# Expert slots for token blocks in groups of 8, 6, 2, 2, 2 and 1, with fewer counting products, later writes of the norms and an earlier read of the diagonal blocks

## The chip, the core and the metric

The kernel runs on one core of a Trainium2 chip. The metric is the time of one execution in device microseconds (us); lower is better. The engines are TensorE (PE; its weight loads are listed as PEld), VectorE (DVE), ScalarE (ACT), GpSimd (POOL) and SyncE (SP), which here only issues DMAs. Each engine runs its instructions in program order.

## The reference, cut to what matters

A delta-rule linear attention runs over 4 batches of 8 heads with 768 steps of width 48. Its output is 3072 tokens of 384 features, and a mixture of 8 experts is applied to them, each token going to the one expert with the largest gate logit.

```python
for t in range(S):
    y[:, :, t] = einsum('bhd,bhde->bhe', q[:, :, t], state)
    v_old = einsum('bhde,bhd->bhe', state, k_n[:, :, t])
    state = state + beta_t * einsum('bhd,bhe->bhde', k_n[:, :, t], v[:, :, t] - v_old)
x = y.transpose(0, 2, 1, 3).reshape(3072, 384)
logits = x @ w_gate
expert_idx = argmax(logits, axis=1)
gate_w = softmax(logits)[arange(3072), expert_idx]
for e in range(8):
    xe = x[expert_idx == e]
    out[expert_idx == e] = gate_w * (relu(xe @ w1[e]) @ w2[e])
```

## The kernel before, in words

**Blocks and ticks.** Time is cut into chunks of 128 steps, so there are NT = 6 chunks of B = 4 batches: NN = 24 blocks of 128 tokens. Block n is batch n % 4 of chunk n // 4. The main loop has 27 ticks. In tick t four lanes of 32 rows work on the blocks t, t-1, t-2 and t-3 (LAG is 3), each on another quarter of its block. `residual(t)` forms key times state on PE and DVE subtracts it from v (L468). `apply(t)` multiplies by the inverse of a triangular 32x32 matrix (L476), and ACT copies the result (L481). `qpart`, `kpart` and `finish` form the other products (L282, L496, L506, L516). PE, ACT and DVE all take part in each tick, and the next tick's residual needs the state that this tick's copies write.

**The inverses.** `prepare(tb)` and `lanes(tb)` compute on DVE the inverses for all blocks of a chunk, some 27 us of DVE work per chunk. Their steps are handed out by `beside(t, i)`, which is called at seven places (i = 0 to 6) in each tick, so their instructions stand in DVE's queue between those that PE waits for. They read the diagonal 32x32 blocks of a Gram matrix: `diagonal` (L251) writes them to DRAM in two parts of four DMAs, and `gather` (L257) reads them back into the tile `lg`. The list `off` says at which tick and place each is issued. The norms that `prepare` gives are turned by DVE and written by four small DMAs (L352) into `nt_t`, which `scale_v` (L426) reads at the end of the chunk before its use, two or more ticks later.

**Slots.** When block n is finished, `emit_x` (tick n + 4, L546) forms its 128 output rows and gate logits in one PSUM bank, and ACT copies the rows to a tile `row` (L547). Blocks are gathered into groups of w: 4 for the blocks 0 to 11, 2 for 12 to 19, and 1 for the last four. `emit_slots` is a generator that takes one step per call. It finds each token's expert on DVE (L565 to L583), counts on PE with a triangular product (L588) and one small product for every pair of blocks in a group (L591), adds the running base on DVE (L597, L598), forms the slot numbers (L610 to L626), writes the rows with one DMA per two blocks to `xn` in token order (L630), and lets POOL scatter each block's rows to its experts' slots in `xg` by an indirect DMA (L640). The list `fine` holds the generators; `beside` steps only the first of them, 17 times per tick. For groups of 4 the scatters go two per tick, at place 3 or later of the two ticks that follow.

**The rest.** From tick 20 on expert weights are loaded and split into two parts of lower precision (L677, L678). After the ticks, from about 310 us on, the experts' products run on PE alone (L789, L799, L1101). Rows of an expert beyond 448 would be done in a loop that these inputs do not enter.

Of the kernel before, what the change touches and what calls it, by code (L numbers as in the profile page):

```python
# [8 lines left out]
F32 = mybir.dt.float32  # L9
F32R = mybir.dt.float32r  # L10
BF16 = mybir.dt.bfloat16
I32 = mybir.dt.int32
# [6 lines left out]
B, H, S, D = 4, 8, 768, 48  # L19
C = 128  # L20
NT = S // C
# [4 lines left out]
E = 8  # L26
# [16 lines left out]
def deltanet_moe(ctx, tc, qT, kT, kr, v, beta, w_gate, w1, w2, out):  # L43
# [30 lines left out]
    def constants():  # L74
        nc.gpsimd.memset(esel, 0.0)
        for p in range(NP):
            for a in range(2):
                r, x = (64 * (a ^ p % 2), a * D)
                nc.gpsimd.tensor_copy(esel[r:r + D, p, x:x + D], ident[r:r + D, r:r + D])
        cmask = lp.tile([128, 128], F32, name="cmask", tag="u", bufs=UB)  # L80
        nc.gpsimd.memset(cmask, 1.0)
        nc.gpsimd.affine_select(out=cmask, in_=cmask, compare_op=ALU.is_gt, fill=0.0, base=0,
                                pattern=[[1, 128]], channel_multiplier=-1)
        nc.gpsimd.tensor_copy(ltri, cmask)
        nc.gpsimd.memset(ones, 1.0)
# [4 lines left out]
        iota(ids, [[-C, B * NT]], int(TOPID), -1)  # L90
# [21 lines left out]
    FINE = (3, 3, 3, 2, 2, 2, 2)  # L112
    W0 = 42
    WD = {1: 12, 2: 15, 3: 14, 4: 3}
    W1 = 4
    W4 = 12
    DM2 = 0
    DEF = 2
    AH = 3
# [139 lines left out]
    def put_off(at, tb, b):  # L259

        if tb == 1:
            diagonal(tb, b)
            if b == B - 1:
                gather(tb)
            return
        off.append((at, lambda: diagonal(tb, b)))
        if b == B - 1:
            off.append(((at[0], 3), lambda: gather(tb)))

    def due(t, i):  # L270

# [44 lines left out]
    def prepare(tb):  # L316
# [168 lines left out]
    def finish(n):  # L485
# [33 lines left out]
        for j in range(2):  # L519
            nc.scalar.copy(out=yt[:, j::2], in_=yp[j])  # L520
        yield
        w = 1 if n >= NN - W1 else 2 if n >= W4 else 4
        j, m = n % w, min(w, 2)
        if j == 0:
            tiles["rows"] = []
            tiles["rl"] = lp.tile([128, w, E], F32, name=f"rl{tb}_{b}", tag=f"rl{w}", bufs=2)
        if j % m == 0:
            pool, tag = (fp, "rowb") if j >= 2 else (rp, "row") if n < NN - 2 else (xq_[0], "row")
            t = pool.tile([128, 2 if n < NN - 2 else 1, ROW], F32, name=f"row{tb}_{b}", tag=tag, bufs=2)
            tiles["rows"].append(t[:, 0:m])  # L530
        xp = emit_x(n, yt, tiles["rows"][-1][:, j % m])
        yield
        nc.vector.tensor_reduce(out=tiles["rl"][:, j], in_=xp[:, :, 2 * D:].rearrange("t p e -> t e p"), axis=AX.X, op=ALU.add)
        if j == w - 1:
            fine.append(emit_slots(tb, b - w + 1, w, tiles["rows"], tiles["rl"]))

    def st_view(b, p):
        t = st_t[b][0:RP, p, :]
# [11 lines left out]
    def emit_slots(tb, b, w, parts, rl):  # L550

        V = nc.vector

        def small(nm, shape, dt=F32):
            return lp.tile(shape, dt, name=f"{nm}{tb}_{b}", tag=f"{nm}{w}", bufs=1 if w > 1 else 2)

        def wide(t):
            return t.unsqueeze(2).broadcast_to([128, w, E])
# [8 lines left out]
        m = w // len(parts)  # L567

        def span(i):
            return slice((b + i * m) * NT + tb, (b + i * m + m - 1) * NT + tb + 1, NT)  # L570
# [4 lines left out]
        cols = slice(b * NT + tb, (b + w - 1) * NT + tb + 1, NT)  # L575
        oh = small("oh", [128, w, E])
        V.scalar_tensor_tensor(out=oh, in0=lm, scalar=0.0, in1=both(rev_e), op0=ALU.is_ge, op1=ALU.mult)
        yield
# [14 lines left out]
        dst = xg if tb * B + b < NN - DEF else xt  # L593
# [10 lines left out]
        if tb * B + b + w == NN - DEF:  # L604

            V.scalar_tensor_tensor(out=base, in0=lim, scalar=float(128 * NG - CAP), in1=base, op0=ALU.add, op1=ALU.max)
        if tb * B + b + w == EU:
# [11 lines left out]
        yield  # L619
        if dst is xt:  # L620

            one = rp.tile([128, CAP - 128 * NG], F32, name=f"one{b}")
            V.tensor_scalar(out=one, in0=last_i, scalar1=sl_all[:, cols], scalar2=None, op0=ALU.is_equal)
            last.append((parts[0][:, 0], one))
        sli = rp.tile([128, w], I32, name=f"sli{tb}_{b}", tag=f"sli{w}", bufs=2)
        V.tensor_copy(sli, sl_all[:, cols])  # L626
        yield
        t1 = t0
        def keep(i):
            nc.sync.dma_start(out=xn.rearrange("(b t p) c -> t p b c", b=B, p=C)[tb, :, b + i * m:b + i * m + m], in_=parts[i])  # L630

        keep(0)
        for j in range(w):
            if w > 1 and j % 2 == 0:
                while tiles["t"] == t1 or tiles["at"] < (2 if w == 2 else 3):
                    yield
                t1 = tiles["t"]
                if j > 0:
                    keep(j // m)
            ins = nc.gpsimd.indirect_dma_start(out=dst, out_offset=bass.IndirectOffsetOnAxis(ap=sli[:, j:j + 1], axis=0),  # L640
                                         in_=parts[j // m][:, j % m], in_offset=None, bounds_check=E * CAP - 1, oob_is_err=False)
            for x in put:
                tc.declare_no_dep(ins.ins, x, reason="slots are distinct rows")
            if w > 1 and j % 2 == 0:
                after(ins, "behind the small products", tiles["few"])
            put.append(ins.ins)
        if tb * B + b + w == EU:
            load_main(0, 0, G0)
        if tb * B + b + w == NN - DEF:
            load_main(0, G0, NG)  # L650

    def run(gen, steps=1):
# [305 lines left out]
    def beside(t, i):  # L958

        tiles["t"], tiles["at"] = t, i  # L960
        due(t, i)
        inverses((STEPS0 if t < B else STEPS)[i], t, i)
        if before and (t, i) >= READY.get(before[0][0], (B * before[0][0] - B, 0)):
            if not run(before[0][1], 3):
                before.pop(0)
        for _ in range(FINE[i] if t < NN - B else 4):
            if fine and not run(fine[0]):
                fine.pop(0)
        for _ in range(WSL.count((t, i))):
            run(W)  # L970
        for _ in range(ES.count((t, i))):
            ahead_step()
# [334 lines left out]
```

## Time and profile before

| | us |
|---|---|
| runs | 525.05, 533.33, 526.01 |
| median | 526.01 |
| the profiled execution, its own time | 532.47 |
| its span, first to last instruction | 530.7 |
| mean granted clock of TensorE in it, of full speed | 0.961 |

Times in the rows below count from the span's start. A row of a timeline, of the chain of waits or of the stretches comes from that one execution, which is 6.46 us above the median of the three runs. Line numbers are those of the kernel before.

### The profile page before, as it was taken

How to read it: one execution, taken by the hardware profiler on the slowest of the kernel's cores; microseconds unless marked ns; L12 is line 12 of the kernel's file. 1: busy time of each engine (PE TensorE's matmuls, PEld its weight loads, DVE VectorE, ACT ScalarE, POOL GpSimd, SP SyncE). 2: the span in 40 equal slices, each digit the busy share in tenths (PEclk: the TensorE clock that was granted, in tenths of full speed). 3: DMA queues.
4: the chain of work that ended last, by engine and by line, in shares of the span. 5: the costliest groups of instructions: out<-in, count | busy, mean ns of one | idle time of the engine just before them, and what ended most of it. 6: DMA issues, size and time to landing. Idle time of an engine off the chain costs nothing.

```text
span 530.7 us, 17441 instructions
## 1 busy us (share of the span) xinstructions
PE 487.4 (92%) x7298; PEld 435.4 (82%) x7298; DVE 344.3 (65%) x1013; ACT 253.8 (48%) x536; POOL 113.1 (21%) x146
## 2 busy tenths in 40 slices
PE   7899999998998978888999899999999999999992
PEld 5755678787887867767888799999999999999991
DVE  2999869798899996455432775565665645575310
ACT  3512557574866736564441454444545434454310
POOL 6010111242331524042122010303021130303111
PEclk8699999998999989798999989999999999999997
DMA  6588738756676455465122667483754638481000
GB/s 214 125 219 249 182 119 219 201 159 177 200 189 182 140 173 149 150 198 145 49 88 90 155 198 174 129 203 123 168 159 131 174 109 180 119 202 62 13 18 26
DMA packets 78317, 79.10 MB, mean 149 GB/s; under 512 B 46985, under 2 KB 65978, under 8 KB 78236
## 3 DMA queue, kind: packets, MB, share of 16 engines
q1 hardware_dynamic: 74780, 68.39, 48.1%
q0 software_dynamic: 3456, 9.57, 4.9%
q8 instruction: 58, 0.95, 0.8%
q14 instruction: 23, 0.19, 0.1%
HBM read 54.25 MB, written 24.37 MB: 148 GB/s over the span
## 4 chain that ended last, share of the span: by engine, by line
PE 60%; DVE 26%; issue 3%; ACT 3%; DMA 3%; SPq 2%; POOL 1%; ACTq 0%; DVEq 0%; POOLq 0%
PE h L789 21%; PE y L799 18%; DVE lw L383 7%; PE y L1101 4%; DVE ta L372 4%; DVE tc L393 3%; PE pq L282 2%; PE xp L546 2%; DVE tc L401 2%; PE ks L476 2%; PE ks L449 2%; PE yp L516 2%; DVE tb L372 2%; PE pg L282 2%; SPq L717 1%
## 5 line engine op out<-in xcount | busy, mean ns | idle before, releaser
L799 PE MATMUL y<-w2h,hx 128*128 128x384 f32 x352 | 93.8, 340 | 2.3 <-DVE hx L793 2.1
L802 POOL DMA_INDIRECT out_dram<-yo,idx x32 | 40.3, 1260 | 203.8 <-ACT yo L1096 116.2
L799 PEld LDWEIGHTS y<-w2h,hx 128*128 128x128 f32 x352 | 64.1, 188 | 3.9 <-DVE hx L793 3.0
L678 DVE TENSOR_TENSOR w2l<-w2r,w2h 128x768 fp32r<-128x768 f32 x32 | 31.4, 983 | 48.6 <-ACT w2h L677 48.1
L481 ACT COPY u<-ks 32x384 f32<-32x384 f32 x96 | 45.1, 469 | 35.0 <-PE ks L476 28.6
L789 PE MATMUL h<-xh,w1l 128*128 128x448 f32 x168 | 61.4, 366 | 0.0
L789 PE MATMUL h<-xl,w1h 128*128 128x448 f32 x168 | 61.3, 365 | 0.0
L789 PE MATMUL h<-xh,w1h 128*128 128x448 f32 x168 | 61.2, 364 | 0.0
L799 PE MATMUL y<-w2l,hx 128*128 128x384 f32 x176 | 59.5, 338 | 0.0
L793 DVE SCALAR_TENSOR_TENSOR hx<-h,hx 128x448 fp32r<-128x448 f32 (+1 forms) x64 | 37.5, 587 | 29.2 <-ACT hx L792 28.5
L792 ACT ACTIVATE hx<-h 128x448 fp32r<-128x448 f32 (+1 forms) x64 | 33.2, 518 | 46.8 <-PE h L789 46.8
L301 POOL TENSOR_SCALAR_AFFINE_SELECT pm<-pm 128x1024 f32<-128x1024 f32 x24 | 27.3, 1136 | 115.6 <-DVE tb L372 35.9
L449 PE MATMUL ks<-st,kt 112*32 112x96 f32 x768 | 43.0, 249 | 1.8 <-issue 1.5
L1096 ACT ACTIVATE yo<-y,gt 128x384 f32<-128x384 f32 x22 | 12.8, 581 | 63.3 <-PE y L799 36.2
L678 DVE TENSOR_TENSOR w1l<-w1r,w1h 128x1024 fp32r<-128x1024 f32 x24 | 29.5, 1230 | 13.3 <-ACT w1h L677 12.8
L449 PEld LDWEIGHTS ks<-st,kt 112*32 112x32 f32 x768 | 31.9, 110 | 6.5 <-issue 2.6
L383 DVE TENSOR_TENSOR lw<-lw,ta 128x31 f32<-128x31 f32 (+7 forms) x96 | 36.7, 382 | 0.2
L476 PE MATMUL ks<-v_all,wt 32*32 32x48 f32 x1536 | 25.9, 209 | 11.3 <-DVE v_all L468 8.4
L476 PEld LDWEIGHTS ks<-v_all,wt 32*32 32x32 f32 x1536 | 21.6, 109 | 17.0 <-DVE v_all L468 11.6
L282 PE MATMUL pg<-kt 48*128 48x128 f32 x384 | 32.3, 317 | 3.2 <-DMA kt<-in_kT_dram 2.0
L547 ACT COPY row<-xp 128x384 f32<-128x384 f32 x24 | 11.5, 479 | 48.3 <-PE xp L546 48.3
L282 PEld LDWEIGHTS pg<-kt 48*128 48x128 f32 x384 | 28.5, 221 | 6.6 <-ACT gg L241 2.3
(162 smaller groups left out, 1055.5 us busy)
## 6 DMA issues: line engine op xcount, KB each, us to landing
w1r<-in_w_dram SPq DMA_DIRECT2D x24, 512.0 KB
w2r<-in_w_dram SPq DMA_DIRECT2D x32, 384.0 KB
xg<-zrow SPq DMA_DIRECT2D x14, 394.0 KB
kt<-in_kT_dram SPq DMA_DIRECT2D x24, 224.0 KB
qt<-in_qT_dram SPq DMA_DIRECT2D x24, 224.0 KB
xr<-xg SPq DMA_DIRECT2D x28, 168.0 KB
xn<-row SPq DMA_DIRECT2D x10, 394.0 KB
ku<-in_kr_dram SPq DMA_DIRECT2D x20, 192.0 KB
```

The source lines that it names most:

```text
L282: ins = nc.tensor.matmul(pg[a][:, p], lhsT=kt[r, p], rhs=xt[r, p], start=True, stop=True, tile_position=(64 * a, 0), skip_group_check=True)
L372: noted(nc.vector.tensor_tensor(out=x, in0=lg[:, rows, c:c + 1].broadcast_to([128, m, w]), in1=lw[:, c:c + 1, cols].broadcast_to([128, m, ...
L383: tiles["mark"] = noted(nc.vector.tensor_tensor(out=y, in0=y, in1=x, op=ALU.subtract))
L449: nc.tensor.matmul(ks[32 * q:32 * q + 32, 2 * p:2 * p + 2, :], lhsT=kt_t[n % KTL][0:RP, p, 32 * q:32 * q + 32], rhs=st_view(n % B, p), sta ...
L476: ins = nc.tensor.matmul(ks[r, h, :], lhsT=tiles[n // B]["wt"][r, n % B * H + h, :], rhs=vn[r, h, :], start=True, stop=True, tile_position ...
L481: nc.scalar.copy(out=uview(n)[r], in_=ks[r])
L678: nc.vector.tensor_tensor(out=lo, in0=src, in1=hi.bitcast(F32), op=ALU.subtract)
L789: nc.tensor.matmul(ps, lhsT=w[:, d, fs], rhs=x_[:, d], start=(n == 0), stop=(n == len(terms) - 1))
L792: nc.scalar.activation(out=hh, in_=ps, func=AF.Relu)
L793: nc.vector.scalar_tensor_tensor(out=hl, in0=ps, scalar=0.0, in1=hh.bitcast(F32), op0=ALU.max, op1=ALU.subtract)
L799: nc.tensor.matmul(ps, lhsT=h(f)[h_], rhs=w2[w][:, f, :], start=(n == 0), stop=(n == len(terms) - 1))
L802: nc.gpsimd.indirect_dma_start(out=out, out_offset=bass.IndirectOffsetOnAxis(ap=idx, axis=0), in_=yo, in_offset=None, bounds_check=N - 1, ...
```

## The change

Five things are edited.

- The blocks are grouped as 8, 6, 2, 2, 2, 1, 1, 1, 1. The groups of 4 that ended with the blocks 3 and 11 are gone; the group that ends with block 7 has eight blocks, the one that ends with block 13 has six. A group may now span two or more chunks, so the columns of `ids`, `sl_all` and `m2_all` are ordered by block. The rows of a group's third and later blocks go to tiles `row1`, `row2`, `row3` with one buffer each, in place of one tile with two buffers.
- Counting takes w products behind the triangular one: product i adds the counts of block i to all later columns at once, by a broadcast operand.
- The scatters of the group of 8 go two per tick in four ticks, those of the group of 6 three per tick in two ticks from place 2 on. `beside` steps all generators in `fine`, not only the first.
- For the chunks from 2 on the four writes of the norms go to `off`, for place 2 of tick 4 tb - 3, instead of being issued as soon as `prepare` ends in tick 4 tb - 4.
- `gather` is issued at place 2 of its tick instead of place 3.

```diff
-    W1 = 4
-    W4 = 12
+    GROUPS = (8, 6, 2, 2, 2, 1, 1, 1, 1)
...
-            off.append(((at[0], 3), lambda: gather(tb)))
+            off.append(((at[0], 2), lambda: gather(tb)))
...
-            for q in range(NB):
-                p = slice(32 * q, 32 * q + 32)
-                nc.sync.dma_start(out=nt_t[p, (B * tb + q) * H:(B * tb + q) * H + 32], in_=sn[p])
+            def spread():
+                for q in range(NB):
+                    p = slice(32 * q, 32 * q + 32)
+                    nc.sync.dma_start(out=nt_t[p, (B * tb + q) * H:(B * tb + q) * H + 32], in_=sn[p])
+
+            if tb < 2:
+                spread()
+            else:
+                off.append(((B * (tb - 1) + 1, 2), spread))
+                off.sort(key=lambda x: x[0])
...
-            pool, tag = (fp, "rowb") if j >= 2 else (rp, "row") if n < NN - 2 else (xq_[0], "row")
-            t = pool.tile([128, 2 if n < NN - 2 else 1, ROW], F32, name=f"row{tb}_{b}", tag=tag, bufs=2)
+            pool, tag = (lp, f"row{j // 2}") if j >= 2 else (rp, "row") if n < NN - 2 else (xq_[0], "row")
+            t = pool.tile([128, 2 if n < NN - 2 else 1, ROW], F32, name=f"row{tb}_{b}", tag=tag, bufs=1 if j >= 2 else 2)
...
-        for j in range(1, w + 1):
-            for i in range(j):
-                nc.tensor.matmul(pp[:, j, :], lhsT=ones, rhs=ohb[:, i], start=False, stop=(i == j - 1),
-                                 skip_group_check=True)
+        for i in range(w):
+            nc.tensor.matmul(pp[:, i + 1:w + 1, :], lhsT=ones, rhs=ohb[:, i:i + 1].broadcast_to([128, w - i, E]), start=False,
+                             stop=(i == w - 1), skip_group_check=True)
...
+        few = 3 if w == 6 else 2
         for j in range(w):
-            if w > 1 and j % 2 == 0:
-                while tiles["t"] == t1 or tiles["at"] < (2 if w == 2 else 3):
+            if w > 1 and j % few == 0:
+                while tiles["t"] == t1 or tiles["at"] < (2 if n0 >= w else 3):
                     yield
                 t1 = tiles["t"]
-                if j > 0:
-                    keep(j // m)
+            if j > 0 and j % m == 0:
+                keep(j // m)
...
-            if fine and not run(fine[0]):
-                fine.pop(0)
+            for g in list(fine):
+                if not run(g):
+                    fine.remove(g)
```

## Rows read from the trace of the kernel before

**Rows 1.** The page, part 4: shares of the chain that ended last.

```profile
PE 60%; DVE 26%; issue 3%; ACT 3%; DMA 3%; SPq 2%; POOL 1%; ACTq 0%; DVEq 0%; POOLq 0%
```

**Rows 2.** Stretches (ticks 10, 15, 16): length, busy of each engine, clock, DMA share, GB/s.

```profile
120.80:131.20 10.40, 8.59 (x225) 7.53 (x226) 8.57 (x25) 5.22 (x12) 2.90 (x4) 0.84 0.64 152
...
164.50:172.00 7.50, 6.33 (x222) 5.52 (x223) 7.19 (x21) 4.86 (x15) 1.45 (x2) 1.00 0.60 191
172.00:179.30 7.30, 6.99 (x220) 6.08 (x219) 6.92 (x35) 4.72 (x12) 3.44 (x4) 1.00 0.39 128
```

**Rows 3.** Groups of instructions by shape: a slot step on DVE, the counting products.

```profile
L612 DVE SCALAR_TENSOR_TENSOR pos<-ovr,pos 128x16 f32<-128x16 f32 x4 | 0.7, 172 | 0.1
...
L612 DVE SCALAR_TENSOR_TENSOR pos<-ovr,pos 128x32 f32<-128x32 f32 x3 | 0.6, 192 | 0.1
...
L591 PE MATMUL xp<-ohb,ones 128*128 128x8 bf16 x46 | 2.7, 166 | 0.0
```

**Rows 4.** Chain of waits in tick 7: start, us, what.

```profile
97.82 0.12 PE xp L588
97.94 0.24 PE xp L591 x10
```

**Rows 5.** Timeline of DVE and ACT in tick 8.

```profile
105.21 0.19 DVE L326 TENSOR_SCALAR ss<-lg 128x32 f32<-128x32 f32 x1 [2.28 <-DMA lg<-gd]
105.43 0.23 ACT L329 ACTIVATE s<-ss 128x32 f32<-128x32 f32 x1 [1.56 <-DVE ss L326]
```

**Rows 6.** Timeline of the SP queue, ticks 7 and 12.

```profile
93.09 1.86 SPq L251 DMA_DIRECT2D gd<-gg  x4
...
98.46 0.34 SPq L257 DMA_DIRECT2D lg<-gd  x1
...
143.94 2.45 SPq L352 DMA_DIRECT2D nt_all<-sn  x4
```

**Rows 7.** Chain of waits in ticks 15 and 16: the slot steps of blocks 8 to 11.

```profile
166.78 0.20 DVE mx L565
...
171.38 0.16 DVE base L598
...
173.52 0.25 DVE sli L626
```

**Rows 8.** Timeline of PE in ticks 15 and 16.

```profile
167.92 0.19 PE L588 MATMUL xp<-ohb,ltri 128*128 128x32 bf16 x1 [0.25 <-DVE ohb L583]
...
171.69 1.11 PE L546 MATMUL xp<-esel,yt 128*128 128x104 f32 x8 [0.32 <-DVE ovr L610]
```

**Rows 9.** Timeline of POOL, ACT and PE, ticks 13 to 15.

```profile
151.46 1.03 POOL L640 DMA_INDIRECT xg<-row,sli  x1 [0.31 <-issue]
...
157.48 1.94 ACT L481 COPY u<-ks 32x384 f32<-32x384 f32 x4 [1.23 <-PE ks L476]
...
165.10 0.88 PE L476 MATMUL ks<-v_all,wt 32*32 32x48 f32 x64 [0.79 <-DVE v_all L468]
```

**Rows 10.** Line L640, tick 13: landing of its two scatters.

```profile
DMA to landing us min/median/max: 6.4/6.6/6.8
```

**Rows 11.** Chain of waits in ticks 10 and 11.

```profile
122.08 1.24 issue
...
124.31 1.98 PE pq L282 x16
...
133.56 1.09 PE pq L282 x16
```

**Rows 12.** The page, parts 1 and 3: instructions of each engine; the instruction queue.

```profile
PE 487.4 (92%) x7298; PEld 435.4 (82%) x7298; DVE 344.3 (65%) x1013; ACT 253.8 (48%) x536; POOL 113.1 (21%) x146
...
q8 instruction: 58, 0.95, 0.8%
```

**Rows 13.** Stretches as in rows 2: between two PE gaps; ahead of the second.

```profile
103.90:123.25 19.35, 16.73 (x509) 14.45 (x508) 17.38 (x78) 11.24 (x27) 7.00 (x8) 1.00 0.67 194
...
117.50:121.00 3.50, 2.75 (x89) 2.43 (x88) 3.50 (x17) 1.56 (x4) 0.00 (x0) 1.00 0.94 311
```

More of the change, by code (lines that the diff above doesn't have):

```diff
@@ L89, in constants @@
         iota(lim, [[CAP, E]], CAP)
-        iota(ids, [[-C, B * NT]], int(TOPID), -1)
+        iota(ids, [[-C, NT], [-C * NT, B]], int(TOPID), -1)
         nc.gpsimd.memset(ids2, 0.0)
@@ L521, in finish @@
         yield
-        w = 1 if n >= NN - W1 else 2 if n >= W4 else 4
-        j, m = n % w, min(w, 2)
+        w, j = [(w, j) for w in GROUPS for j in range(w)][n]
+        m = min(w, 2)
         if j == 0:
@@ L534, in finish @@
         if j == w - 1:
-            fine.append(emit_slots(tb, b - w + 1, w, tiles["rows"], tiles["rl"]))
+            fine.append(emit_slots(n - w + 1, w, tiles["rows"], tiles["rl"]))
     def st_view(b, p):
@@ L548, in emit_x, with emit_slots @@
         return xp
-    def emit_slots(tb, b, w, parts, rl):
-        V = nc.vector
+    def emit_slots(n0, w, parts, rl):
+        V, n1 = nc.vector, n0 + w
         def small(nm, shape, dt=F32):
-            return lp.tile(shape, dt, name=f"{nm}{tb}_{b}", tag=f"{nm}{w}", bufs=1 if w > 1 else 2)
+            return lp.tile(shape, dt, name=f"{nm}{n0}", tag=f"{nm}{w}", bufs=1 if w > 1 else 2)
         def wide(t):
@@ L569, in span @@
         def span(i):
-            return slice((b + i * m) * NT + tb, (b + i * m + m - 1) * NT + tb + 1, NT)
+            return slice(n0 + i * m, n0 + i * m + m)
         lm = small("lm", [128, w, E]) if len(parts) > 1 else parts[0][:, :, DM:DM + E]
@@ L574, in emit_slots @@
         yield
-        cols = slice(b * NT + tb, (b + w - 1) * NT + tb + 1, NT)
+        cols = slice(n0, n1)
         oh = small("oh", [128, w, E])
@@ L588, in emit_slots @@
         nc.tensor.matmul(pp[:, 0:w, :], lhsT=ltri, rhs=ohb, start=True, stop=False, skip_group_check=True)
[L589 to L593 removed]
+        for i in range(w):
+            nc.tensor.matmul(pp[:, i + 1:w + 1, :], lhsT=ones, rhs=ohb[:, i:i + 1].broadcast_to([128, w - i, E]), start=False,
+                             stop=(i == w - 1), skip_group_check=True)
+        dst = xg if n0 < NN - DEF else xt
         pos, ovr = small("pos", [128, w, E]), small("ovr", [128, w, E])
@@ L603, in emit_slots @@
             nc.scalar.copy(out=row[:, :, DM + E:ROW], in_=ids2[:, span(i)])
-        if tb * B + b + w == NN - DEF:
+        if n1 == NN - DEF:
             V.scalar_tensor_tensor(out=base, in0=lim, scalar=float(128 * NG - CAP), in1=base, op0=ALU.add, op1=ALU.max)
-        if tb * B + b + w == EU:
+        if n1 == EU:
             V.scalar_tensor_tensor(out=base, in0=lim, scalar=float(128 * G0 - CAP), in1=base, op0=ALU.add, op1=ALU.max)
@@ L620, in emit_slots @@
         if dst is xt:
-            one = rp.tile([128, CAP - 128 * NG], F32, name=f"one{b}")
+            one = rp.tile([128, CAP - 128 * NG], F32, name=f"one{n0}")
             V.tensor_scalar(out=one, in0=last_i, scalar1=sl_all[:, cols], scalar2=None, op0=ALU.is_equal)
             last.append((parts[0][:, 0], one))
-        sli = rp.tile([128, w], I32, name=f"sli{tb}_{b}", tag=f"sli{w}", bufs=2)
+        sli = rp.tile([128, w], I32, name=f"sli{n0}", tag=f"sli{w}", bufs=2)
         V.tensor_copy(sli, sl_all[:, cols])
@@ L629, in keep @@
         def keep(i):
-            nc.sync.dma_start(out=xn.rearrange("(b t p) c -> t p b c", b=B, p=C)[tb, :, b + i * m:b + i * m + m], in_=parts[i])
+            t, b = divmod(n0 + i * m, B)
+            nc.sync.dma_start(out=xn.rearrange("(b t p) c -> t p b c", b=B, p=C)[t, :, b:b + m], in_=parts[i])
         keep(0)
+        few = 3 if w == 6 else 2
         for j in range(w):
-            if w > 1 and j % 2 == 0:
-                while tiles["t"] == t1 or tiles["at"] < (2 if w == 2 else 3):
+            if w > 1 and j % few == 0:
+                while tiles["t"] == t1 or tiles["at"] < (2 if n0 >= w else 3):
                     yield
                 t1 = tiles["t"]
-                if j > 0:
-                    keep(j // m)
+            if j > 0 and j % m == 0:
+                keep(j // m)
             ins = nc.gpsimd.indirect_dma_start(out=dst, out_offset=bass.IndirectOffsetOnAxis(ap=sli[:, j:j + 1], axis=0),
@@ L643, in emit_slots @@
                 tc.declare_no_dep(ins.ins, x, reason="slots are distinct rows")
-            if w > 1 and j % 2 == 0:
+            if w > 1 and j % few == 0:
                 after(ins, "behind the small products", tiles["few"])
             put.append(ins.ins)
-        if tb * B + b + w == EU:
+        if n1 == EU:
             load_main(0, 0, G0)
-        if tb * B + b + w == NN - DEF:
+        if n1 == NN - DEF:
             load_main(0, G0, NG)
```

## Prediction

> **What bounds the kernel now.** I read the page's chain of work first: 60% of the span ends on PE, 26% on DVE, 3% on PE waiting for nothing that the profile shows ("issue") [rows 1]. The experts' stage after the ticks is PE alone and nothing of it is edited, so whatever the change brings arises in the ticks and is then carried to the end as a shift. Next I cut the ticks into stretches, to see which engine is full in each. In ticks 15 and 16 DVE is busy 7.19 of 7.50 and 6.92 of 7.30 us, PE 6.33 and 6.99 [rows 2]: DVE leads, and PE has 1.2 and 0.3 us to spare. There the chain goes through the inverses and through the slot steps between them [rows 7]. In ticks 7 and 8 the chain runs on PE, through the counting products [rows 4], and DVE has time left. So a slot step saved on DVE counts around tick 15 and not around tick 7, and a product saved on PE counts around tick 7 and not around tick 15. A third view is the list of who waits, for what is late next: in tick 8 DVE waits 2.28 us for the diagonal blocks and ACT 1.56 us behind it [rows 5].
>
> **The change part by part.** The sums are against the profiled execution, 532.47 us of its own time for a span of 530.7 us. That is 6.46 us above the median of 526.01, so some of its stalls may be its own; I carry the differences to the median and say where that is doubtful.
>
> *The group of blocks 0 to 3 goes (ticks 7 and 8).* PE loses one triangular and ten counting products, 0.12 + 0.24 = 0.36 us of the chain [rows 4], 24 ns each for the small ones. DVE's twelve steps there are beside PE's chain and worth nothing. But what is late next is the read of the diagonal blocks, for which DVE stands until 105.21 and ACT's copies of tick 8 behind it [rows 5]. The read was issued at 98.46, long after the four writes of 93.09 [rows 6], because it waits for them to land. Placed earlier it waits for the same landing, so I give the earlier place almost nothing, and the 0.36 us of the products is mostly eaten by this wait. I take -0.2 for both, between 0 and -1.2 (0.36, plus half of the 1.56 us that ACT stands).
>
> *The group of blocks 8 to 11 goes (ticks 15 and 16).* Its steps lie on the chain as eleven pieces: five of the kind of the first (0.20 at 166.78), four from 171.38 that take 0.72, two of which the last begins at 173.52 [rows 7]; together 2.02 us. DVE can't use all of it, for PE must be ready too. PE waited 0.25 us for the expert's marks, spent 0.36 us on products as in tick 7, and had its residual finished 0.32 us ahead of 171.69 while DVE came to the subtraction at 171.38 + 0.72 = 172.1 [rows 4, 7, 8]. So PE allows 0.25 + 0.36 + (172.1 - 171.37) = 1.34 us, and in tick 16 another 0.31 us, its spare time there [rows 2]. I take -1.6, between -1.3 and -2.0.
>
> *The group at tick 17 grows from two blocks to six.* A DVE step costs 172 ns at 16 elements and 192 at 32 [rows 3], so 20 ns for each 16; 48 elements cost 40 ns more than 16, in ten steps 0.4 us, where DVE leads. Three more products (24 ns each) and five more ACT copies lie beside DVE. I take +0.4, between +0.3 and +0.6.
>
> *The group at tick 11 grows from four to eight.* By the same slope 40 ns in ten steps, 0.4 us on DVE, which is covered as PE leads in ticks 11 and 12; 9 products replace 11, and four more copies stand ahead of ACT's other work. Nothing, and +0.9 at most if that cover is gone.
>
> *The groups of two behind it* lose one product each: 3 x 24 ns, -0.1.
>
> *The tile of blocks 2 and 3 now has one buffer.* It is used again by block 10 in tick 14, one tick after its two scatters (place 3 of tick 13) and its write to `xn`. Before, at the same place of tick 13, the second scatter was issued at 151.46, and the two landed after 6.4 and 6.8 us [rows 9, 10]: at up to 158.3. ACT's row copy of tick 14 can then start only there, and in ACT's queue the copies of u, which started at 157.48, stand behind it [rows 9]. They would be 0.8 us late and the row copy's own time more; it has the columns of one of the four copies in 1.94 us, so 0.5, and 1.3 in all. The cover is DVE's lead: PE stands 0.79 us for it in tick 15 before L476 [rows 9]. I take +0.3, between 0 and +1.3. SP's later writes of the norms (below) also put this group's write to `xn` later.
>
> *The norms' writes move a tick later.* The four DMAs took 2.45 us of SP's queue at 143.94 [rows 6]. At the new place they stand ahead of the tick's load of q, of the group's write to `xn`, of the load of k and of the next diagonal writes. All of these are used a tick or more later, and the norms themselves two ticks later. Nothing, between 0 and +0.4.
>
> *Stepping all generators.* At most two are alive together (ticks 18 to 20), and one of them then only waits for a tick. POOL issues three scatters in a row in ticks 18 and 19, about 1.3 us each by the pace of rows 9, and each tick is longer than that. Nothing.
>
> Sum: -0.2 - 1.6 + 0.4 - 0.1 + 0.3 = -1.2 us; at the bounds -3.1 and +1.8. The profiled execution would come out at 531.3, the median at **524.8 us** (522.9 to 527.8).
>
> **The rivals.**
>
> *A stall of PE in tick 10 goes too.* PE stands 1.24 us at 122.08 in the midst of equal products, waiting for nothing that is shown, and then runs at half speed: 1.98 us for 16 products that take 1.09 a tick later [rows 11]. The clock of that tick is 0.84 on average over 10.40 us, which is 3.3 us at 1.2 GHz in place of 2.4 [rows 2] and costs up to 1.65. What PE waits for can be read from counts. 58 packets bring 0.95 MB of instructions, 16 KB each, and PE's 7298 loads and 7298 products make about 252 to a packet [rows 12]. From the end of the stall in tick 8 to the end of this one PE ran 509 loads and as many products [rows 13], 1018, four packets within 1%. So this looks like a packet of instructions that came late, and just ahead of it the DMA engines were 0.94 busy [rows 13]. Two scatters and a write to `xn` of the group that goes fall into tick 9; without them the packet would come sooner. Against it: the stall may be missing from the faster executions already, and the diagonal writes and loads stay. It would give 1.24 + 1.65 = 2.9 us more than the sum: 521.9. The Trainium skill speaks against this rival: its page "Runtime: NRT & Kernel Launch", section "Instruction fetch mechanics", has the next 16 KiB fetched while the current one runs and calls the cost of a block's boundary mostly hidden. By that rule the stall is no matter of packets, the traffic would not change it, and the sum would stay at 524.8.
>
> *The same stall appears in ticks 14 and 15: slower.* The scatters and writes taken from ticks 9, 16 and 17 go to ticks 14, 15, 18 and 19. Ticks 14 and 15 would each carry two scatters and a write of two blocks' rows more, on top of the four diagonal writes. If a packet is then late by as much as in tick 10, each tick pays 2.9 us less the 0.79 us for which PE waits on DVE anyway, 2.1; two ticks 4.2. With the sum that is 526.0 - 1.2 + 4.2 = 529.0, slower than before. It decides from the point at which the DMA share ahead of a packet reaches that of rows 13, 0.94. For it speaks the amount of data, against it that DVE leads here and that tick 15 had a share of only 0.60 [rows 2].
>
> *The earlier read does nothing.* It waits for the landing of the diagonal writes and is issued at the same moment; DVE's and ACT's waits of tick 8 remain in full, and swallow the products saved there. That gives the sum without its first term, 525.0. The change would then be the regrouping of the slots alone.
>
> **How the numbers follow.** The forecast, that the slot steps of tick 15 are what is saved, gets 0.5 at 524.8; the stall of tick 10 gone 0.25 at 521.9; stalls in ticks 14 and 15 0.15 at 529.0; the earlier read without any effect 0.10 at 525.0. The range takes in the first, the second with a little of its lower bound, and the third: 520.5 to 530.0. Two per cent, 10.5 us, is about what a measurement of this kernel can tell from no change; the three runs alone lie 8.3 us apart. No case reaches 515.5 or 536.5 by itself. I leave 0.05 to each side for several stalls that come or go together: no change 0.90.
>
> **What would show it.** The chain of ticks 15 and 16 without slot steps, tick 15 shorter by about a microsecond; tick 17 longer by some 0.4. In tick 8 the wait of DVE for `lg` near 2.3 us still, and SP's issue of that read hardly sooner after the diagonal writes than 98.46 - 93.09 = 5.4 us. In tick 14 ACT waiting ahead of the row copy for a DMA, and PE's wait for DVE in tick 15 smaller than 0.79. For the rivals: in tick 10 no "issue" piece and a clock of 1.00, or such pieces in ticks 14 and 15 with DMA shares of 0.94 and more ahead of them. The prediction would be wrong if DVE's saving in tick 15 were given back as PE waiting for ACT or for a packet, or if the wait for row tile 1 reached past DVE's lead.

## The result: half a per cent to one per cent slower

The changed kernel takes 534.16 us (median of 20 runs, 530.61 to 542.55), the kernel before 531.61 us (524.40 to 536.87) in as many runs beside it: 2.55 us more, 0.5%; the means lie 3.7 us apart, 0.7%. The ratio, 1.0096 with an interval of [1.0067, 1.0125], compares fast runs alone, those within 1.5% of the fastest of their kernel (19 of 20 changed, 11 of 20 before), and so lies above that of the medians. It stands for some 5 us, and the ratios below are of the same kind. By each of these figures the kernel is slower, and by less than two per cent.

The median of 526.01 on which the forecast was built came from three runs; it is 5.6 us below that of twenty. Of the 9.4 us between the forecast of 524.8 and 534.16, this base makes up 5.6; the rest is the change itself, +2.55 us where -1.2 was forecast. From 526.01 the ratio would give 531.1, above the range, and the ratio of the medians, 1.0048, would give 528.5, inside it; the direction was wrong by either.

The profiled execution of the changed kernel took 536.5 us, its span 534.8. First the page's shares of the chain that ended last, against [rows 1]:

```profile
PE 63%; DVE 19%; DMA 6%; ACT 4%; issue 3%; SPq 2%; POOL 1%; POOLq 0%; ACTq 0%; DVEq 0%
```

DVE ends 7% less of the span than before, PE 3% more and DMA 3% more. Some two of DMA's three per cent are two pieces of 5.6 us, from 195.21 and 204.86 on, that go through a write to `xn`: it landed just as DVE and ACT, neither of them idle, began another instruction, so they are no stall. Next the stretches of ticks 10, 15, 16, 18 and 19 of the changed kernel (columns as in [rows 2]), and the 4 us up to PE's last weight load ahead of a gap in tick 16:

```profile
118.80:127.40 8.60, 8.02 (x235) 6.87 (x233) 8.53 (x26) 5.72 (x14) 1.45 (x2) 1.00 0.83 182
160.90:168.10 7.20, 5.87 (x209) 5.06 (x210) 5.56 (x11) 4.38 (x11) 4.63 (x6) 1.00 0.54 137
168.10:177.90 9.80, 7.17 (x217) 6.00 (x218) 6.07 (x31) 4.71 (x12) 1.71 (x3) 1.00 0.60 201
188.75:197.82 9.07, 8.47 (x209) 7.45 (x210) 8.85 (x26) 4.11 (x10) 5.05 (x5) 0.62 0.54 165
197.82:205.01 7.19, 6.97 (x222) 6.12 (x222) 6.86 (x21) 4.69 (x12) 4.89 (x5) 1.00 0.62 193
...
165.91:169.91 4.00, 4.00 (x165) 3.50 (x162) 1.57 (x5) 2.15 (x7) 2.45 (x3) 1.00 0.94 319
```

Tick 10 has lost its slow stretch: 8.60 us at a clock of 1.00, where [rows 2] has 10.40 at 0.84. In tick 15 DVE fell from 7.19 to 5.56 us busy, but the tick only from 7.50 to 7.20. Tick 16 grew from 7.30 to 9.80 us with neither PE nor DVE full. Ticks 18 and 19 carry three scatters each, POOL's 5.05 and 4.89 us; tick 18 ran at a clock of 0.62, so mostly at 1.2 GHz, after a stretch of 3 us (186.00 to 189.00) in which PE was busy 1.11; before, it had 0.88 there. The two together took 16.26 us against 16.19 before. Where the time of ticks 15 and 16 goes is in their chain of waits:

```profile
161.48 0.54 PE ks L483 x32
162.03 0.75 issue
162.78 0.54 PE ks L483 x31
...
169.91 0.37 PE yp L503 x6
170.29 2.41 issue
172.70 0.59 PE yp L503 x10
```

PE stands 0.75 us and then 2.41 us in the midst of equal products, waiting for nothing that the profile shows, as it did before in tick 10 [rows 11]. Three more lines of the changed kernel's timelines answer to [rows 5, 6, 9]: DVE's wait for the diagonal blocks, SP's issue of their read in tick 7, and ACT's wait ahead of the row copy of tick 14.

```profile
103.04 0.19 DVE L325 TENSOR_SCALAR ss<-lg 128x32 f32<-128x32 f32 x1 [1.18 <-DMA lg<-gd]
...
92.22 1.98 SPq L250 DMA_DIRECT2D gd<-gg  x4
...
98.14 0.34 SPq L256 DMA_DIRECT2D lg<-gd  x1
...
153.42 0.48 ACT L554 COPY row<-xp 128x384 f32<-128x384 f32 x1 [3.08 <-DMA xn<-row]
```

A tick's length below is the distance between the first subtractions of two ticks (L468 before, L475 after). Over ticks 7 to 25 the changed kernel is 3.11 us longer: 3.42 shorter in ticks 7 to 10, 0.17 longer in 11 to 14, 2.25 in 15 and 16, -0.35 in 17 to 19, and 4.46 in 20 to 25. One execution of each says little about that last figure, as will be seen.

### The profile page after: what moved, and what is told of

The parts are those of the page before. It is cut to its first block, busy times and chain, and to the rows that moved or that the text cites. A ratio compares the mean times of both kernels' runs of the same rounds, so it can differ in the third digit from the quotient of the medians.

```text
span 534.8 us, 17348 instructions
## 1 busy us (share of the span) xinstructions
PE 489.2 (91%) x7268; PEld 436.7 (82%) x7274; DVE 340.2 (64%) x989; ACT 254.2 (48%) x537; POOL 114.9 (21%) x146
## 4 chain that ended last, share of the span: by engine, by line
PE 63%; DVE 19%; DMA 6%; ACT 4%; issue 3%; SPq 2%; POOL 1%; POOLq 0%; ACTq 0%; DVEq 0%
PE h L797 21%; PE y L807 18%; DVE lw L390 5%; PE y L1110 4%; DVE ta L379 3%; PE ks L456 3%; PE pq L281 3%; PE ks L483 3%; DVE tc L400 2%; DMA xn<-row 2%; PE pg L281 2%; PE xp L553 2%; DMA kt<-in_kT_dram 2%; PE ks L468 2%; PE wm L679 2%
## 5 line engine op out<-in xcount | busy, mean ns | idle before, releaser
L456 PE MATMUL ks<-st,kt 112*32 112x96 f32 x768 | 44.6, 255 | 0.4 <-ACT st L517 0.3
L1105 ACT ACTIVATE yo<-y,gt 128x384 f32<-128x384 f32 x22 | 12.8, 581 | 63.4 <-PE y L807 36.1
L456 PEld LDWEIGHTS ks<-st,kt 112*32 112x32 f32 x768 | 33.3, 112 | 5.1 <-issue 1.6
L797 PEld LDWEIGHTS h<-xh,w1l 128*128 128x128 f32 x168 | 31.6, 188 | 2.9
```

The costliest lines, as they stand in the source:

```text
L456: nc.tensor.matmul(ks[32 * q:32 * q + 32, 2 * p:2 * p + 2, :], lhsT=kt_t[n % KTL][0:RP, p, 32 * q:32 * q + 32], rhs=st_view(n % B, p), sta ...
L797: nc.tensor.matmul(ps, lhsT=w[:, d, fs], rhs=x_[:, d], start=(n == 0), stop=(n == len(terms) - 1))
```

## The experiments

The letters in the expectations stand for theories. P: the lost products shift where PE's packets of instructions begin. T: the data moved into ticks 14 and 15, the writes to `xn` among it, holds a packet up. N: the later norms and the earlier read do. S: the group of eight's scatters there do. L: the loads of tick 15 do. R, later R2: a tick with more than two scatters costs by itself. An issue piece or a gap is a stretch in which PE waits for nothing that the profile shows.

**Packets at their old places.** Small products make up for those lost, so that packets begin at the same products as before.

```diff
+    PADS = {7: 11, 11: 2, 15: 11}
...
+        if i == 3 and t in PADS:
+            pd = tiles["bank"][:, 504:512]
+            for _ in range(PADS[t]):
+                nc.tensor.matmul(pd, lhsT=ones, rhs=busy[:, 0:8], start=False, stop=True, skip_group_check=True)
```

> The changed kernel with 24 tiny products (8 columns, into free columns of the bank) added at place 3 of the ticks 7, 11 and 15 (11, 2 and 11), so that PE's instructions stand at the same count as in the kernel before at nearly every tick, and the packets of instructions begin at the same products. Theory P (the place where packets begin decides where PE stands): the stall of 2.4 us in tick 16 of the changed kernel goes, and the time is that of the kernel before or up to 3 us less (ratio 0.994 to 1.001). Theory T (the data moved to the ticks 14 to 16 and 18 to 20 makes packets late, wherever they begin): a stall of 1 to 3 us stays in the ticks 15 to 17, and the ratio is 1.006 to 1.012 as for the whole change.

Measured: ratio 1.0107 [1.0063, 1.0150]; tick 16 took 13.30 us, with a gap of 3.38 us in its chain. P falls.

**No writes to `xn`** (the rows in token order are left out).

```diff
-            nc.sync.dma_start(out=xn.rearrange("(b t p) c -> t p b c", b=B, p=C)[t, :, b:b + m], in_=parts[i])
+            pass
```

> The changed kernel without the writes of the rows in token order to xn, which only the loop for more than 448 rows reads (left out: 14 DMAs, 4.7 MB). Theory T: with this data gone the packets come in time, no stall over 0.8 us in the ticks 8 to 19, and the ratio to the kernel before falls to 0.990 or less. Theory P: the packets begin at the same products as in the changed kernel, the stall of tick 16 stays, ratio 1.003 to 1.010.

Measured: 1.0069 [1.0033, 1.0104]; the gap in tick 16 stayed, 3.10 us, and the tick took 11.64. T falls.

**The norms and the read alone, and the slots alone.** The first is the kernel before with the changed `norms` and `gather` at place 2; the second is the changed kernel with these two as before.

```diff
-            off.append(((at[0], 3), lambda: gather(tb)))
+            off.append(((at[0], 2), lambda: gather(tb)))
...
+                off.append(((B * (tb - 1) + 1, 2), spread))
```

> The kernel before with only the norms' writes a tick later and the diagonal blocks' read at place 2. PE's instructions are those of the kernel before. Theory P: the same as before, ratio 0.997 to 1.003. Theory T as I hold it (only the rows' data matters): the same as well. A third theory, N, that the norms' writes delay the tick's other loads and so make the loss: ratio 1.005 or more.

> The changed kernel with the norms' writes and the diagonal blocks' read back in their old places, so only the groups and the products are changed. Theories P and T: the loss is all here, ratio 1.006 to 1.012, with a stall of PE of 1.5 us or more in one of the ticks 14 to 17. Theory N: ratio 0.995 to 1.002.

Measured: 1.0009 [0.9974, 1.0045] and 1.0109 [1.0065, 1.0152]. N falls; the loss lies in the slots.

**The counting products alone**, in the kernel before.

```diff
-        for j in range(1, w + 1):
-            for i in range(j):
...
+        for i in range(w):
+            nc.tensor.matmul(pp[:, i + 1:w + 1, :], lhsT=ones, rhs=ohb[:, i:i + 1].broadcast_to([128, w - i, E]), start=False,
+                             stop=(i == w - 1), skip_group_check=True)
```

> The kernel before with w counting products per group in place of one for every pair, and nothing else changed. By the price of 24 ns a product, 6 fewer in each group of 4 on PE's chain: 0.15 us each, ratio 0.998 to 1.001. Theory P would allow stalls elsewhere and a ratio up to 1.008.

Measured: 1.0035 [1.0002, 1.0068], above the 0.998 to 1.001 that the price of 24 ns a product gave. They save nothing that shows; if anything they cost a little, by an interval that only just clears 1. Most of what is lost goes with the groups and their scatters.

**Scatters in tick 15.** Three kernels: the group of eight passes over tick 15 (scatters in 12, 13, 14 and 16); it goes four at a time in ticks 12 and 13; and the kernel before scatters two rows more, to a tensor that nothing reads, in tick 15.

```diff
-                while tiles["t"] == t1 or tiles["at"] < (2 if n0 >= w else 3):
+                while tiles["t"] == t1 or tiles["at"] < (2 if n0 >= w else 3) or (w == 8 and tiles["t"] == 15):
...
-        few = 3 if w == 6 else 2
+        few = 3 if w == 6 else 4 if w == 8 else 2
...
+        if tb * B + b == 4:
+            while (tiles["t"], tiles["at"]) < (15, 3):
+                yield
+            for j in range(2, 4):
+                ins = nc.gpsimd.indirect_dma_start(out=xg2, ...)
```

> The changed kernel with the scatters of the group of 8 in the ticks 12, 13, 14 and 16, none in tick 15. Theory S (the two scatters of tick 15 stand in the DMA engines ahead of the packet of instructions that PE needs in tick 16): the stall of 2.4 to 3.4 us in tick 16 shrinks below 1 us, and the ratio to the kernel before falls to 0.996 to 1.003. Theory L (the loads of tick 15 and 16 themselves, the diagonal blocks, q, k and v, make the packet late, since DVE reaches them earlier): the stall stays at 2 us or more and the ratio at 1.006 to 1.012.

> The changed kernel with the scatters of the group of 8 four per tick, in the ticks 12 and 13, so none in 14 and 15. Theory S: as before, no stall over 1 us in tick 16, ratio 0.996 to 1.003, unless four in a row make a packet late in tick 13 (then a stall there). Theory L: stall in tick 16 of 2 us or more, ratio 1.006 to 1.012.

> The kernel before with two scatters more: the rows of blocks 6 and 7 are scattered once again at place 3 of tick 15, to a scratch tensor that nobody reads. Theory S: PE stalls in tick 16 for 1.5 us or more, tick 16 takes 9 to 13 us in place of 7.3, ratio 1.004 to 1.010. Theory L: no stall over 1 us in tick 16, ratio 0.998 to 1.003.

Measured: 1.0060 [1.0020, 1.0101], 1.0183 [1.0127, 1.0239] and 0.9990 [0.9952, 1.0028]. The gap in tick 16 was there in the first two (1.47 and 2.50 us; tick 16 9.67 and 10.15), and the third had 8.55 us and a gap of 0.42. S falls, though 1.47 is also less than the 2 us or more that L expected. But the second showed something new: ticks 12 and 13, with four scatters each, took 11.53 and 13.48 us, against 7.73 and 9.02 in the changed kernel. R was formed on that.

**The groups 8, 4, 2, 2, 2, 2, 1, 1, 1, 1**: blocks 8 to 11 are a group again, and no tick has more than two scatters.

```diff
-    GROUPS = (8, 6, 2, 2, 2, 1, 1, 1, 1)
+    GROUPS = (8, 4, 2, 2, 2, 2, 1, 1, 1, 1)
```

> Groups of 8, 4, 2, 2, 2, 2, 1, 1, 1, 1: the group of blocks 0 to 3 stays merged into the one of eight, but blocks 8 to 11 are a group of their own again, as before, with two scatters in each of the ticks 16 and 17. So DVE's eleven steps are back in tick 15, nothing is scattered three at a time, and ticks 7 to 11 stay as in the changed kernel. Theory L (the stall of tick 16 comes because PE, freed of the slot steps, crosses into a new packet while the loads of tick 15 fill the DMA engines; before, the slot steps held it back): tick 15 back to about 7.5 us, tick 16 between 7.3 and 9.3 as in the four runs with the groups of before, against 9.7 to 13.3 in the six with the new groups; ticks 18 and 19 together about 16.2 against 16.3 to 18.9; ratio 0.990 to 1.000. Rival (the two scatters of the group of eight in tick 15, or the packets' phase after the lost products, make the stall): tick 16 stays over 9.7 with an issue piece of 1.8 us or more, and the ratio is 1.003 to 1.008.

Measured: 0.9988 [0.9947, 1.0029], although the gap stayed (1.64 us, tick 16 11.84). Neither theory foresaw both: the slot steps in tick 15 don't hold the stall off, and without the group of six the loss is gone, stall or not.

**The loads of tick 15 behind the work of tick 16**, in the changed kernel.

```diff
     def load(out, in_):
+        if tiles.get("t") == 15:
+            off.append(((16, 4), lambda: nc.sync.dma_start(out=out, in_=in_)))
...
+            return
...
     def clear_slots(n=1):
+        if tiles.get("t") == 15:
+            return
...
```

> The changed kernel with the loads of tick 15 (q, k, v and the clearing of one piece of the slots; some 0.6 MB) issued behind the tick's other work at place 4 of tick 16; the read of the diagonal blocks, the group's write and its two scatters stay in tick 15. Theory L: the packet for tick 16 no longer queues behind them, so the issue piece of tick 16 falls from 1.8 to 3.6 us to under 1, tick 16 takes 7.3 to 8.5 us, and the ratio falls by 0.5% or more, to 1.002 to 1.006 (the cost of ticks 18 and 19 stays). If the read of the diagonal blocks (0.5 MB) is enough by itself to hold the packet up, or if the traffic isn't the cause, tick 16 stays over 9.5 and the ratio is 1.007 to 1.012.

Measured: 1.0091 [1.0053, 1.0129]; tick 16 took 7.92 us with a gap of 0.55. The 4 us up to PE's last weight load ahead of it:

```profile
165.19:169.19 4.00, 3.63 (x147) 3.12 (x144) 1.08 (x5) 1.88 (x6) 1.48 (x3) 1.00 0.74 269
```

The DMA share is 0.74 where the changed kernel had 0.94. So far L; but the ratio didn't follow (L expected 1.002 to 1.006), and the run with the same edit below contradicts it.

**The third scatter of ticks 18 and 19 held back** to place 5.

```diff
+            while w == 6 and j % 3 == 2 and tiles["at"] < 5:
+                yield
```

> The changed kernel with the third scatter of the ticks 18 and 19 held back to place 5 of its tick, so that POOL issues two in a row and one by itself. Theory R (while POOL issues a third scatter in a row, PE's products come 0.4 us apart; seen in tick 19 of five of the six runs with the new groups and, with four in a row, in ticks 12 and 13): tick 19 about 7.2 us in place of 8.4 to 8.5, and the ratio falls by 0.2%, to about 1.007; tick 16 as in the changed kernel. If the third scatter isn't what slows PE there, tick 19 stays at 8.4.

Measured: 1.0108 [1.0055, 1.0162], tick 19 8.71 us. No gain, and not much of a test: POOL began the third scatter of tick 19 1.47 us behind the second, and 1.79 us behind it without the edit, so the edit held nothing apart.

**The kernel before with all four scatters of a group in one tick.**

```diff
-            if w > 1 and j % 2 == 0:
+            if w > 1 and j % w == 0:
```

> The kernel before with all four scatters of a group of four in one tick (8, 12 and 16) in place of two and two. Theory R: each of these ticks has issue pieces of PE beside the third and the fourth scatter and becomes 2 to 5 us longer, as the ticks 12 and 13 did where the group of eight went four at a time; the ticks after them (9, 13, 17), which lose their scatters, gain at most 0.4; ratio 1.010 to 1.025. If the cost there came from the eight blocks' data and not from the row of four, under 1 us each and a ratio of 1.000 to 1.004.

Measured: 1.0205 [1.0155, 1.0256]. Tick 8 took 11.62 us (9.15 before), tick 12 12.48 (7.81), tick 16 12.16 (7.25). R as expected, in the groups of before: this and the four at a time above are the clearest losses of all.

**Two scatters per tick for the group of six** (ticks 18, 19 and 20; those of blocks 14 and 15 in tick 21), without and with the loads of tick 15 later.

```diff
-        few = 3 if w == 6 else 2
+        few = 2
+        while n0 == 14 and tiles["t"] < 21:
+            yield
```

> The changed kernel with the six scatters of the group of six two at a time in the ticks 18, 19 and 20, and those of blocks 14 and 15 in tick 21, so that no tick has more than two. Theory R2 (the rest of the loss is the three scatters per tick, their data and the row of three): ticks 18 and 19 together 16.2 to 16.8 in place of 17.9 to 18.9, and the ratio falls to about 1.003, with tick 16's stall still there. Rival (the group of six costs by its wider steps or its place, not by its scatters): the ratio stays at 1.007 to 1.012.

> As the run before it, and the loads of tick 15 at place 4 of tick 16 as well. If both theories hold and add, tick 16 takes 7.3 to 8.5 us, ticks 18 and 19 at most 16.8, and the ratio is 0.994 to 1.000. If the loads' place is worth nothing in the median, it equals the run before it within 0.2%.

Measured: 1.0020 [0.9977, 1.0064] and 1.0012 [0.9969, 1.0055]. Most of the loss is gone, and ticks 18 and 19 of the first took 16.81 us, as R has it; the edit also moves the scatters of blocks 14 and 15 from tick 20 to 21, so it isn't the third scatter alone that was taken away. The later loads add nothing, and the second kernel, which up to tick 16 is the program that had a gap of 0.55 us above, has one of 2.13 here. The 4 us up to PE's last weight load ahead of the gap, and its chain:

```profile
165.33:169.33 4.00, 4.00 (x165) 3.50 (x162) 2.21 (x5) 2.17 (x7) 2.43 (x3) 1.00 0.97 316
```

```profile
169.71 2.13 issue
```

**The later loads with the groups 8, 4, 2, ... and with those of before**: the edit of the groups and that of the loads, put together, and the second on the kernel before.

```diff
+    GROUPS = (8, 4, 2, 2, 2, 2, 1, 1, 1, 1)
...
+            off.append(((16, 4), lambda: nc.sync.dma_start(out=out, in_=in_)))
```

> Groups of 8, 4, 2, 2, 2, 2, 1, 1, 1, 1 with the loads of tick 15 at place 4 of tick 16. That grouping alone came out at 0.999 with 11.84 us for tick 16; if the stall there is what swallows the gain of the ticks 7 to 10, tick 16 takes at most 8.5 us and the ratio is 0.991 to 0.996. If not, 0.997 to 1.001.

> The kernel before with the loads of tick 15 at place 4 of tick 16. There tick 16 had 7.3 to 9.3 us and issue pieces under 1.5, so little is to be had: 0.997 to 1.002 by either theory. A gain like that of the run before it would say that these loads cost every grouping, and not the changed one more.

Measured: 1.0008 [0.9965, 1.0050] with 8.30 us for tick 16, and 1.0042 [1.0002, 1.0082], where tick 16 took 7.50 us against 7.25 before and tick 17 15.33 in place of 11.25. With a group of eight, moved loads shortened tick 16 in two kernels of three; the median gained nothing clear of noise in any of the four.

**All six scatters in tick 18; and the kernel before with the three scatters of ticks 18 and 19** (four more, to tensors that nothing reads).

```diff
-        few = 3 if w == 6 else 2
+        few = 6 if w == 6 else 2
...
+        if w == 2 and tb * B + b == 12:
+            for k in range(4):
+                if k == 1:
+                    while (tiles["t"], tiles["at"]) < (19, 2):
+                        yield
+                ins = nc.gpsimd.indirect_dma_start(out=xg2 if k < 2 else xg3, ...)
```

> The changed kernel with all six scatters of the group of six in tick 18 and none in tick 19. Theory R2 (a tick with more than two scatters costs, and the more the more): tick 18 becomes 4 to 8 us longer, tick 19 loses its 1.3 us, and the ratio rises from 1.010 to 1.013 to 1.020. Rival (the loss comes from the group's steps and place): 1.007 to 1.011, as in the changed kernel.

> The kernel before with four scatters more, one in tick 18 behind the two that are there and three in tick 19, of the rows of blocks 12 and 13 to tensors that nothing reads: the ticks 18 and 19 then carry three scatters each as in the changed kernel, with the groups, the counting products and all else as before. Theory R2: ticks 18 and 19 together 17.5 to 19 us in place of 16.2, and a ratio of 1.003 to 1.009. Rival (three scatters cost only together with the group of six): 0.998 to 1.002 and ticks 18 and 19 within 0.4 us of before.

Measured: 1.0109 [1.0039, 1.0180], with tick 18 at 14.34 us; and 1.0032 [0.9996, 1.0069], with 19.28 us for ticks 18 and 19 against 16.19 before. The six cost their tick 5 us, as R2 has it, but the median no more than the three did: 1.0109 is what the rival, the group's steps and place, expected, and not the 1.013 to 1.020 of R2. The second kernel shows the price of three scatters in their ticks, with the groups of before; in the median it is in R2's range, but the interval reaches 1. Its timeline of POOL and its chain in tick 18:

```profile
195.77 0.99 POOL L642 DMA_INDIRECT xg<-row,sli  x1 [2.05 <-PE sb L508]
197.07 1.38 POOL L642 DMA_INDIRECT xg<-row,sli  x1 [0.31 <-issue]
198.75 1.24 POOL L654 DMA_INDIRECT xg<-row,sli  x1 [0.30 <-issue]
```

```profile
197.36 0.08 PE ks L463 x5
197.44 0.43 issue
197.87 0.29 PE ks L463 x3
198.16 0.46 issue
198.62 0.29 PE ks L463 x4
198.91 0.47 issue
199.37 0.28 PE ks L463 x4
199.65 0.46 issue
```

From the second scatter to the end of the third PE does three or four products, stands 0.45 us, and so on: 1.82 us in four gaps.

## Why the prediction was wrong

Single executions differ by several us in where PE stalls, so the ticks are set side by side as means: A over four kernels with the groups of before (before, the norms and read alone, the products alone, two more scatters in tick 15), B over five with the new groups and three scatters (the changed kernel, packets at old places, no `xn`, tick 15 passed over, the third held back), C over two with the group of eight and at most two scatters (8, 4, 2, ...; two each).

| mean us of ticks | 7-10 | 11-14 | 15-16 | 17-19 | 20-25 | all |
|---|---|---|---|---|---|---|
| A | 36.07 | 34.69 | 15.88 | 26.96 | 61.61 | 175.21 |
| B | 33.03 | 34.10 | 17.85 | 28.59 | 64.67 | 178.24 |
| C | 32.90 | 34.68 | 18.33 | 27.23 | 61.13 | 174.26 |

B is 3.0 us above A, C 0.9 below; the ratios of the kernels in B are 1.006 to 1.011, of those in C 0.999 and 1.002. The spread within A is 58.6 to 63.4 us in ticks 20 to 25, so the last difference there is the least sure. Two things follow. The stall of ticks 15 and 16 stands in C as in B, so it isn't what makes B slower than C; it costs both some 2 us against A, less than the 3 us that both gain in ticks 7 to 10. And of the 4.0 us between B and C 1.4 lie in ticks 17 to 19, where the third scatters are, and 3.5 in ticks 20 to 25, where no tick has three: those are not explained.

- **The products and the read (-0.2): too small.** Tick 7 took 7.42 us against 8.14, and 7.42 to 7.74 in the other kernels of B against 8.06 and more in A. DVE waited 1.18 us for the diagonal blocks, not 2.28 [rows 5]. The read was issued 5.92 us after the writes, no sooner than the 5.37 of [rows 6], and alone it gave 1.0009: the third rival is right as to the read, but the products weren't swallowed.
- **The slot steps of tick 15 (-1.6): the saving was made on DVE and given back on PE.** DVE's 1.63 us came out as forecast, the tick's didn't, which lost only 0.3: PE stood 0.75 us in the midst of equal products in tick 15, and 2.41 in tick 16. That is the failed step: the term of -1.6 took it that PE would use what DVE gave back, up to the 1.34 us that its waits for DVE allowed, and had no wait of PE's own in it. Where PE didn't stand in tick 15 (scatters passed over it, four at a time, two each) the tick took 6.28 to 6.59 us, 0.9 to 1.2 less than before, and tick 16 of the same kernels 9.67 to 10.62 against 7.25. In place of -1.6 ticks 15 and 16 came out at +2.25. The prediction named this as what would make it wrong ("given back as PE waiting ... for a packet").
- **The group of six (+0.4): right.** Tick 17 took 10.83 or 10.84 us in the kernels with it and 10.54 or 10.55 in the two that have the group of eight without it, +0.3. The group of eight cost tick 11 0.13.
- **Row tile 1 (+0.3): nothing.** ACT waited 3.08 us for the write to `xn`, but it was back by 153.42; tick 14 is 8.57 us in both kernels. The tile's two scatters, expected to land at up to 158.3, were down by 150.9 (issued at 146.38 and 147.84, 4.0 and 3.0 us to landing). The lower bound held.
- **Norms (0): right**, by the kernel that has them and the read alone.
- **"Three scatters in a row ... Nothing": wrong**, and the other failed step. The argument counted POOL's time (three times 1.3 us fit into a tick); what they cost is on PE. By the added scatters it is 3.1 us in ticks 18 and 19 of one execution, and 1.0032 in the median with an interval that reaches 1; two in each tick gave 1.0020. In the changed kernel's own profile these two ticks are no longer than before, in the other four kernels of B they are 17.85 to 18.39 us.
- **The bounds** add up to -3.0, not -3.1; nothing hangs on it.
- **First rival (tick 10's stall goes): it went, but it was seldom there.** Ticks 10 of 8.56 to 8.78 us stand in the three other kernels of A too, and 12.67 in the last run. The stretch of tick 10 moved as much with a share of 0.83 in 8.60 us as before with 0.64 in 10.40, so it isn't the traffic taken away that ended it.
- **Second rival (a late packet where the data went): the late packet was right, the place and the cause were not.** It foresaw ticks 14 and 15 and blamed the scatters there. The stall came in tick 16, in nine of nine profiles with a group of eight and unmoved loads (1.85 to 3.94 us from one of PE's weight loads to the next, against 0.02 to 1.47 in seven with the groups of before), with or without scatters in tick 15. Its condition, a share of 0.94 ahead of the packet, was met in the changed kernel; but the kernel before, by its stretch of 4 us ahead of the like place in tick 16, has 1.01 there and only 0.55 us from one weight load to the next, so the share alone doesn't decide:

```profile
169.20:173.20 4.00, 3.68 (x141) 3.21 (x141) 3.86 (x9) 1.83 (x9) 0.94 (x1) 1.00 1.01 356
```

That these gaps are waits for instructions can be read from the trace, which lists the packets of the instruction queue (q8, 16 KB each). The block of 256 instructions that ends at the gap of the changed kernel began at 167.08; the next packet moved only from 170.34 to 171.38, and PE went on at 172.70. In the kernel before, the like block began at 169.84, and the packet moved from 171.33 to 172.25. Below are the stretches from the block's start to the packet's, changed and before, and the packet of the changed kernel (DMA queues from 170.34 to 171.38):

```profile
167.08:170.34 3.26, 3.21 (x139) 2.65 (x132) 1.38 (x5) 1.35 (x5) 1.28 (x2) 1.00 0.99 359
...
169.84:171.33 1.49, 1.49 (x80) 1.32 (x74) 1.49 (x2) 0.86 (x5) 0.00 (x0) 1.00 0.99 375
...
q8 instruction: 1, 0.02, 6.2%
```

The packet itself takes about a microsecond; late is its start, and until then the DMA engines are full, for 3.26 us in the one kernel and 1.49 in the other. In the nine profiles it began 2.2 to 4.4 us after its block, and PE went on 1.25 to 1.48 us behind its landing; in the seven it began 0.3 to 2.5 us after it.

By the Trainium skill, "Runtime: NRT & Kernel Launch", section "Instruction fetch mechanics", the next block of instructions is fetched while the current one runs, and its cost is mostly hidden. Six in ten such places in these traces agree (under 0.1 us from one instruction to the next); the 2.41 us of tick 16 don't, nor the 1.24 of [rows 11].

What stays open: why, with the group of eight, more data stands ahead of the packet of tick 16. Moving the loads shortened the gap in two kernels of three and not in the third, which is the same program up to there as the first; neither the count at which packets begin, nor the scatters, nor `xn` explains it. The two equal programs differ in when the data came: in the 2 us before the block began the DMA share was 0.91 with the short gap and 0.58 with the long one, so where PE crosses into the block while a burst has just begun, the packet may stand behind more of it. That was not tested. Nor was it settled how a third scatter slows PE, why six in one tick cost the median no more than three, or what makes ticks 20 to 25 of B longer. So that the changed kernel is slower is shown, and that its saving in tick 15 goes into a late packet; the cause of the whole loss is not.

## What to carry to other kernels

Merging work into bigger groups also bunches its data movement: count the scatters and writes per tick, and keep the rate that the kernel had (here two scatters; four in a tick, in two or three ticks, cost 1.8 to 2.1% of the whole). When an engine that leads is relieved, the gain ends at the next stall of the other one, so read both engines' idle time over the next two ticks, and don't book the whole saving. A stall seen in one execution may belong to that execution: before crediting its removal, look for it in several profiles.

## What the runs showed of the hardware

Counting PE's loads, products and waits for semaphores through the traces, the gaps that are waits for instructions lie at one count, 194 above a multiple of 256 (189 in the seven traces that lack six products); they last from nothing to 3.9 us, and in tick 16 of nine kernels they ended 1.25 to 1.48 us after a packet of 16 KB had landed. The gaps beside a row of scatters are another kind: about 0.45 us every 0.7 us, at any count. Two scatters in a tick that had none cost it little (tick 15 7.74 us against 7.52), three in each of two ticks 3.1 us together, four in one tick 2.5 to 4.9 us, six about 5 us; each of these is one execution.
